# Threshold attention and a bilinear FFN on one core: later batches scored head by head, the FFN's first layer wholly in seven products, and the engines' orders taken from a list scheduler

## The chip, the cores and the metric

The kernel runs on one core of a Trainium2 chip. The core has a matmul engine (TensorE, "PE" in the profile, with its weight loads as "PEld"), a vector engine (VectorE, DVE), a scalar engine (ScalarE, ACT), a general engine (GpSimd, POOL) and an engine that here issues nearly all transfers (SyncE, SP). The metric is device time in microseconds, the median of several runs; lower is better. All data are 32-bit floats.

## The reference

```
scores = q @ k.T / 8                       # per batch b (8) and head h (8); 576 x 576, head size 64
thresh = max(scores, last axis) - tau
scores = where(scores >= thresh, scores, -1e9) - max
attn   = exp(scores); attn = attn / (sum(attn) + 1e-9)
x      = attn @ v, laid out as (8*576) tokens x (8*64) features
a, b   = x @ w_a, x @ w_b                  # 512 -> 1536 each
out    = (a * b) @ w_out                   # 1536 -> 512
```

So there is an attention of 64 heads with a hard threshold below each row's maximum, and after it an FFN on 4608 tokens whose hidden layer is the product of two linear maps.

## The kernel before

**Attention.** Work goes by pairs of heads (`pairs`, 32 of them, four to a batch) and by units: a unit (i, u) is 128 queries of pair i, or, for u = `NT`, the last 64 queries of two pairs. There are 144 units: 18 for the first batch, 126 for the other seven. One turn g of the main loop (a slot) starts unit g. `scores` (L389) multiplies queries by keys for both heads of the pair into two PSUM tiles `sc`, each 128 queries by 576 keys, and VectorE takes the row maxima (`mx`, L411) and the thresholds (`thr`, L412, one instruction for both heads). `weigh` (L422) lets ScalarE compute the exponentials into a room `tw` in SBUF (L431, L432), and VectorE select and sum them (L435). `reciprocal` (L440; L446, L448) and `normalise` (L451, L454) finish the rows. In the next slot `turn_blocks` (L493) transposes the room in 32x32 blocks on VectorE (L498) and posts four transfers that write it to DRAM (`swap`); `turn_back` (L513) posts those that read it back as `wT`. Three slots later `weighted` (L606) multiplies it by v (`product`, L542) and `settle` (L546) copies the result into `xT`: one copy on ScalarE (L549), two on VectorE (L550). The first eight units are transposed on the matmul engine instead (`turn_pe`, L468).

**FFN.** Tokens go in 18 blocks of 256. A matmul is a 64x64 tile of the array, and four of them, one in each quarter of the array, run beside each other; the profile shows each as two instructions, so a set of four is eight instructions. The first layer's 1536 columns are three groups of 512. For a block with four tiles of x (`x`, its copy with the two halves of the partitions exchanged `xS`, and two tiles of sums `xU` made by `x_sums`, L567), a group can be computed as a 2x2 block product by seven products instead of eight (`sevens_of`, L679; `product`, L709, matmuls at L720, 128 wide), which needs sums of weight quarters (`first_sums`, L669, L677). `SEVENS = 2` of the three groups go this way; the third goes through `plain` (L810, L824, 256 wide) piece by piece between the products. Only the last two blocks, those that begin after the attention (`state["over"]`), take all three groups by sevens, with the third group's weight sums in three rooms of `tw` (`last_rooms`). The second layer goes by seven products in 17 blocks (L885), with sums of h (`h_sums`, L861, L853) on GpSimd.

**Order.** The FFN is a generator whose steps `advance` (L969) hands out by columns, a share of a block in each slot (`PORTIONS`), so that FFN work lies between the steps of the attention. `keep_order` (L41) then ties each engine's instructions to the order in which the program wrote them. SP's transfers are posted to a list (`post`, L139) and handed to SP one by one as matmul columns go by (`passed`, L169; `pump`, L152), each behind a matmul.

**Rooms.** PSUM has four tiles of two banks (`banks`, L128) shared by scores, values, both FFN layers and transposes. `tw` has three buffers (`TW_BUFS`). The first slots also convert the weights from DRAM (L298 to L324).

Of the kernel before, what the change touches and what calls it, by code (L numbers as in the profile page):

```python
# [32 lines left out]
PART = 36864  # L33
PORTIONS = (0.3, 0.35, 0.15, 0.2)
RAWS = 4
TW_BUFS = 3
SEVENS = 2
BY_HEAD = 16


def keep_order(tc):  # L41

    last = {}
    for ins in tc.nc.cur_bb.bb.instructions:
        before = last.get(ins.engine)
        if before is not None:
            tc.add_manual_dep(
                ins, before,
                mybir.DependencyInfo(mybir.DependencyClass.NoSync, mybir.DependencyReason.DATA),
                reason="order")  # L50
        last[ins.engine] = ins.name
# [3 lines left out]
def kernel(  # L55
# [61 lines left out]

    def pool(name, bufs, **kw):
        return ctx.enter_context(tc.tile_pool(name=name, bufs=bufs, **kw))
# [32 lines left out]
    def pump(count=1, paced=True):  # L152

        for _ in range(min(count, len(bulk))):
            behind = next(x.name for x in reversed(nc.cur_bb.bb.instructions) if x.engine == mybir.EngineType.PE)
            for n, move in enumerate(bulk.pop(0)[2]):
                moved = nc.sync.dma_start(*move)
                if n == 0 and paced:
                    tc.add_manual_dep(
                        moved.ins, behind,  # L160
                        mybir.DependencyInfo(mybir.DependencyClass.Sync, mybir.DependencyReason.DATA),
                        reason="pace")
# [15 lines left out]
    def load(i, name):  # L178
# [6 lines left out]
        t = work.tile([P, most, Q], FP32, tag=name[0] + "T", bufs=bufs, name=name[0] + "T")[:, 0:n1 - n0]  # L185
        for j in range(2):
            rows = src[b, 2 * hp + j].rearrange("(e n) d -> e n d" if name == "k" else "(n e) d -> e n d", e=Q)
            moves = [(t[(2 * j + h) * Q:(2 * j + h + 1) * Q], rows[:, n0:n1, h * Q:(h + 1) * Q]) for h in range(2)]
            for some in ([moves] if name != "k" else [moves[0:1], moves[1:2]]):
                post((name, i), *some)  # L190
# [45 lines left out]
    for F in range(NF):  # L236
# [4 lines left out]
             "layer": False, "paced": False, "all": False, "turn": 0, "due": NPIECES, "wide": True, "slot": 0, "reading": False, "first": 0}  # L241
# [10 lines left out]
    more_sb = more_u32.bitcast(FP32)  # L252

    def load_weights(limit, engine=nc.sync, most=NPIECES):
# [4 lines left out]
        while most and (len(raws) - len(taken) < limit or extra) and state["loaded"] < state["due"]:  # L259
# [7 lines left out]
            for r, part in enumerate(src):  # L267
# [4 lines left out]
                if behind and r == 0:  # L272
                    tc.add_manual_dep(
# [58 lines left out]
    for _ in range(TW_BUFS):  # L332
        t = work.tile([P, 2 * NB, Q], FP32, tag="tw", bufs=TW_BUFS, name="rows")
        rooms.append(t.rearrange("p n e -> p (n e)")[0:R, 0:ROWS])
    rooms += [sums_sb[0:R, c:c + ROWS] for c in range(0, 5 * ROWS, ROWS)]
# [19 lines left out]
    prepared, scored, weights, turned, whole = {}, {}, {}, {}, {}  # L355
# [3 lines left out]
    last_sums = []  # L359
# [28 lines left out]

    def scores(i, u):  # L389
        qT, kT = prepared[i]["q" if i < HP else "q1" if u > 1 else "q0"], prepared[i]["k"]  # L390
        base = HALF if i >= HP and u > 1 else 0
        sc = [banks(SH, "sc") for _ in range(2)]
        wide = D if u == NT else columns()
# [3 lines left out]
        for c, t, j in each:  # L397
            r = slice(j * D, (j + 1) * D)
            if u < NT:
                m, o, q0 = j, t, u * P + t * D - base  # L400
            else:
                m, o, q0 = t, j ^ t, MAIN - base
                qT, kT = prepared[i + t]["q" if i < HP else "q1"], prepared[i + t]["k"]
            nc.tensor.matmul(sc[m][o * D:o * D + wide, c], qT[r, q0:q0 + wide],  # L404
                             kT[r, c * SH:(c + 1) * SH], start=True, stop=True)
        mx = small.tile([P, 2], FP32, tag="mx", name="mx")
        thr = small.tile([P, 2], FP32, tag="thr", name="thr")
        bias = small.tile([P, 2], FP32, tag="bias", name="bias")
        for j in range(2):
            c = slice(j, j + 1)  # L410
            nc.vector.tensor_reduce(mx[:, c], sc[j], axis=AX.XY, op=ALU.max)  # L411
        nc.vector.tensor_scalar(thr, mx, cut, None, op0=ALU.subtract)  # L412
        scored[i, u] = (sc, thr, bias, mx)

    def rooms_of(i, u):


        t = work.tile([P, 2 * NB, Q], FP32, tag="tw", bufs=TW_BUFS, name="tw")
        whole[i, u] = t
        return [t[:, j * NB:(j + 1) * NB] for j in range(2)]  # L420

    def weigh(i, u):  # L422

        sc, thr, bias, mx = scored.pop((i, u))
        n = len(sc)
        sums = small.tile([P, 2], FP32, tag="sums", name="sums")
        ws = rooms_of(i, u)
        sb = [s.rearrange("p c (n e) -> p c n e", e=Q) for s in sc]
        wb = [w.rearrange("p (c n) e -> p c n e", c=2) for w in ws]
        for j in range(n):  # L430
            nc.scalar.activation(bias[:, j:j + 1], mx[:, j:j + 1], AF.Copy, scale=e_nscale)  # L431
            nc.scalar.activation(wb[j], sb[j], AF.Exp, bias=bias[:, j:j + 1], scale=e_scale)  # L432
        for j in range(n):
            wv = wb[j]
            nc.vector.scalar_tensor_tensor(  # L435
                out=wv, in0=sb[j], scalar=thr[:, j:j + 1], in1=wv,
                op0=ALU.is_ge, op1=ALU.mult, accum_out=sums[:, j:j + 1])
        weights[i, u] = (ws, sums)
# [54 lines left out]
    def turn_blocks(i, u):  # L493

        ws, _ = weights.pop((i, u))
        t = whole.pop((i, u))
        for w in ws:
            nc.vector.transpose(w, w)  # L498
# [47 lines left out]
    def settle(out, pv, c0, c1, others):  # L546
# [3 lines left out]
        two = [nc.vector.tensor_copy(out[c * D:(c + 1) * D, n:2 * n], pv[(1 - c) * D:(2 - c) * D, 1, c0:c1])  # L550
               for c in range(2)]
# [23 lines left out]
    def exchange_blocks():  # L575
        while complete and not state["layer"] and not blocks:
# [5 lines left out]
            blocks.append(((x, xs) + ((x_sums(x), x_sums(xs)) if state["first"] >= 3 * SEVENS else ()), what))  # L582
# [76 lines left out]
    def sums_at(group, m):  # L659
        if group == SEVENS:  # L660
            return last_sums[m]
        return (first_sb, more_sb)[group][:, m * QUARTER:(m + 1) * QUARTER]

    def last_rooms():
        for _ in range(3):
            t = work.tile([P, 2 * NB, Q], FP32, tag="tw", bufs=TW_BUFS, name="s")
            last_sums.append(t.rearrange("p n e -> p (n e)")[:, 0:QUARTER])

    def first_sums(n, group):  # L669

        quarter = [w[:, NG - 1 - group].rearrange("p (z y e) w -> p z y (e w)", z=2, y=2)[:, :, y]
                   for w in (wa_sb, wb_sb) for y in range(2)]
        s1, s2, s4 = (sums_at(group, m).rearrange("p (z w) -> p z w", z=2) for m in range(3))
        a11, a12, a21, a22 = quarter
        out, a, b, op = ((s1, a21, a22, ALU.add), (s2, s1, a11, ALU.subtract), (s4, a12, s2, ALU.subtract),
                         (a21, a11, a21, ALU.subtract))[n]
        nc.gpsimd.tensor_tensor(out, a, b, op=op)  # L677

    def sevens_of(x, hg, plain):  # L679

        def pool(*a, **kw):
            (nc.vector if state["over"] else nc.gpsimd).tensor_tensor(*a, **kw)  # L682

        x, xs, t, ts = x

        everything = plain is None
# [6 lines left out]
        def s(m):  # L693
            return [[sums_at(NG - 1 - g, m)[:, k * CH:(k + 1) * CH] for k in range(HP)] if g >= of_all or everything
                    else None for g in range(NG)]
# [10 lines left out]
        nf = 2 * SEVENS  # L706
        two, one = range(of_all, NG), range(of_all)

        def product(m, out, fresh, last, groups=two):  # L709
            w, moving = products[m]  # L710
            nf = 2 * len(groups)
            left = whole = nf * HP * P
# [18 lines left out]

        (g0, g1), (h0, h1) = ([h[:, :, :, n * P:(n + 1) * P].rearrange("p f r n -> p r f n") for n in range(2)]
                              for h in hg)
        third = [work.tile([P, nf * P], FP32, tag="osb", bufs=OSB_BUFS, name="u3") for _ in range(2)]
        done = P, 0, 0

        if everything:
            last = work.tile([P, nf * P], FP32, tag="osb", bufs=OSB_BUFS, name="u3")
            n1, n2 = 2 * P * len(one), 2 * P * len(two)
            sets = [(two, n2, h0, h1, [t.rearrange("p (f n) -> p f n", n=P) for t in third]),  # L740
                    (one, n1, g0, g1, [last[:, r * n1:(r + 1) * n1].rearrange("p (f n) -> p f n", n=P)
                                       for r in range(2)])]
            pa, pb = {}, {}
            for m in (1, 2, 6, 5, 7, 3, 4):
                for groups, width, o0, o1, u in sets:
                    if m in (1, 2, 5):
                        (pa if m == 1 else pb)[width] = banks(width, "pab")
                    out = (pa if m in (1, 6, 7, 4) else pb)[width]
                    yield from product(m, out, m in (1, 2, 5), m in (2, 3, 4), groups)
                    ps = split(out)  # L750
                    if m in (1, 6):
                        nc.scalar.copy((o0, o1)[m == 6], ps)
                    elif m == 5:
                        for r in range(2):
                            nc.scalar.copy(u[r], ps[:, r])
                    elif m == 7:
                        for r in range(2):
                            nc.vector.tensor_tensor(u[r], u[r], ps[:, r], op=ALU.add)
                    else:
                        o = (o0, o1)[m == 3]  # L760
                        nc.vector.tensor_tensor(o, o, ps, op=ALU.mult if m == 4 else ALU.add)
                    if m == 3:
                        for r in range(2):
                            pool(o1[:, r], o1[:, r], u[r], op=ALU.mult)
                    yield done
            return
        a = banks(nf * P, "pab")
# [458 lines left out]
```

## Time and profile before

| | |
|---|---|
| median of 3 runs | 1419.35 us (1418.83 to 1419.81) |
| span of the profiled execution, the only time shown of it | 1417.0 us |
| busy: PE, PEld, DVE, ACT, POOL | 1370.2, 1229.6, 1013.7, 679.9, 495.7 us |
| mean granted TensorE clock | 0.994 |
| moved by DMA | 223.20 MB, 158 GB/s |
| matmul instructions, 128 wide in L720 / 256 wide in L824 / in L885 | 15232 / 4352 / 5712 |

The span is the time from the first to the last instruction of one execution, in which every busy time above lies. "Busy" is the union of an engine's instructions; for PE it is not the same as work at peak rate, since matmuls are pipelined and their ends are modelled. A group's line names the source line, the engine, the operation and the tiles, then the count, the busy time and the mean of one instruction. The chain of waits follows the work that ended last back to the start.

### The profile page before, as it was taken

The page shows a single profiled execution, that of the slowest core. Times are in us where ns is not written, and L with a number is a line of the kernel's source. Part 1 is how long each engine was busy: PE and PEld are TensorE (multiplying, and loading weights), DVE is VectorE, ACT ScalarE, POOL GpSimd, SP SyncE. Part 2 cuts the span into 40 slices and gives each one's busy share as a digit, 9 for nine tenths or more (in the row PEclk, how much of TensorE's full clock was granted, in tenths as well). Part 3 has the DMA queues.
Part 4 walks back from the last instruction along what each step waited for, and adds up shares of the span by engine and source line. Part 5 has one row for each costly group of instructions (what it writes and reads, how often), then busy time and mean ns, then how long its engine had stood idle before and what let it go on. Part 6 is the DMA issues. An engine that isn't in the chain of part 4 may idle for free.

```text
span 1417.0 us, 76257 instructions
## 1 busy us (share of the span) xinstructions
PE 1370.2 (97%) x33836; PEld 1229.6 (87%) x33836; DVE 1013.7 (72%) x2200; ACT 679.9 (48%) x1245; POOL 495.7 (35%) x678
## 2 busy tenths in 40 slices
PE   6788999999999999999999999999999999999998
PEld 5677579989878887979998999999888899799997
DVE  6898986778777877776767777677777776744424
ACT  5786554545445454545444545454545455431110
POOL 2674541606060606042333324150606060608100
PEclk9999999999999999999999999999999999999999
DMA  9967776667756775666555675567655775550000
GB/s 212 235 193 219 182 214 163 178 153 183 198 135 173 198 188 155 178 156 184 142 134 149 168 193 158 144 160 199 168 144 152 191 201 154 135 152 18 4 19 18
DMA packets 327000, 223.20 MB, mean 158 GB/s; under 512 B 171536, under 2 KB 310800, under 8 KB 326672
## 3 DMA queue, kind: packets, MB, share of 16 engines
q1 hardware_dynamic: 323712, 216.95, 59.2%
q8 instruction: 266, 4.36, 1.3%
q10 hardware_dynamic: 2960, 1.38, 0.4%
q14 instruction: 62, 0.51, 0.1%
HBM read 128.58 MB, written 89.65 MB: 154 GB/s over the span
## 4 chain that ended last, share of the span: by engine, by line
PE 86%; DVE 7%; DMA 3%; issue 2%; SPq 1%; ACT 0%; POOL 0%; DVEq 0%; POOLq 0%; ACTq 0%
PE pab L720 29%; PE po L885 20%; PE pab L824 16%; PE pv L542 10%; PE sc L404 10%; DVE mx L411 2%; DVE tw L498 2%; SPq L144 1%; DMA wT<-swap 1%; DVE tw L435 1%; PE tp L479 1%; DMA raw<-in_moe_w_a_dram 1%; DMA raw<-in_moe_w_b_dram 1%; DVE thr L412 0%; DVE u L790 0%
## 5 line engine op out<-in xcount | busy, mean ns | idle before, releaser
L411 DVE TENSOR_REDUCE mx<-sc 128x1 f32<-128x576 f32 x288 | 204.7, 752 | 125.8 <-PE sc L404 125.4
L454 ACT ACTIVATE tw<-tw,rcp 128x576 f32<-128x576 f32 x272 | 196.5, 770 | 202.3 <-DVE rcp L448 202.3
L682 POOL TENSOR_TENSOR h<-h,u 128x512 f32<-128x512 f32 x28 | 35.2, 1276 | 601.0 <-DVE h L794 426.1
L432 ACT ACTIVATE tw<-sc,bias,scalars 128x576 f32<-128x576 f32 x288 | 239.8, 833 | 10.9 <-PE pab L720 0.4
L435 DVE SCALAR_TENSOR_TENSOR tw<-sc,thr,tw 128x576 f32<-128x576 f32 x288 | 221.5, 799 | 10.4 <-ACT tw L432 9.9
L885 PE MATMUL po<-wo_sb,h 64*64 64x256 f32 x3264 | 205.8, 376 | 1.2 <-DVE h L794 1.1
L498 DVE STREAM_TRANSPOSE tw<-tw 128x576 f32<-128x576 f32 x272 | 194.4, 752 | 0.8 <-ACT tw L454 0.8
L885 PEld LDWEIGHTS po<-wo_sb,h 64*64 64x64 f32 x3264 | 157.0, 133 | 25.7 <-DVE h L794 2.6
L542 PE MATMUL pv<-wT,vm 64*64 64x160 f32 (+3 forms) x5184 | 169.2, 275 | 7.6 <-issue 3.6
L542 PEld LDWEIGHTS pv<-wT,vm 64*64 64x64 f32 x5184 | 157.4, 136 | 19.1 <-issue 9.8
L404 PE MATMUL sc<-kT,qT 64*64 64x288 f32 x2016 | 168.0, 404 | 1.1 <-DVE xt L550 0.5
L853 POOL TENSOR_TENSOR h<-h 128x256 f32<-128x256 f32 x168 | 117.4, 732 | 107.4 <-PE po L885 97.2
L885 PE MATMUL po<-sums_u,h 64*64 64x256 f32 x2448 | 153.4, 376 | 0.7 <-DVE h L832 0.7
L720 PE MATMUL pab<-xU,wb_sb 64*64 64x128 f32 x4352 | 138.0, 269 | 0.4 <-issue 0.3
L720 PEld LDWEIGHTS pab<-xU,wb_sb 64*64 64x64 f32 x4352 | 132.2, 133 | 3.7 <-issue 1.1
L885 PEld LDWEIGHTS po<-sums_u,h 64*64 64x64 f32 x2448 | 117.6, 133 | 19.4 <-DVE h L832 1.3
L404 PEld LDWEIGHTS sc<-kT,qT 64*64 64x64 f32 x2016 | 101.8, 133 | 22.6 <-issue 5.0
L549 ACT COPY xT<-pv 128x128 f32<-128x128 f32 (+1 forms) x68 | 17.7, 260 | 201.8 <-PE pv L542 200.2
L431 ACT ACTIVATE bias<-mx,scalars 128x1 f32<-128x1 f32 x288 | 83.1, 288 | 64.0 <-DVE mx L411 63.7
L550 DVE COPY xT<-pv 64x128 f32<-64x128 f32 (+1 forms) x136 | 38.1, 280 | 91.0 <-PE pv L542 89.7
L720 PE MATMUL pab<-xS,wa_sb 64*64 64x128 f32 x2176 | 101.8, 269 | 0.1
L531 ACT COPY kept<-po 128x512 f32<-128x512 f32 x65 | 34.8, 536 | 123.0 <-PE po L885 113.9
(156 smaller groups left out, 2414.3 us busy)
## 6 DMA issues: line engine op xcount, KB each, us to landing
wT<-swap SPq DMA_DIRECT2D x244, 288.0 KB, 3.9
swap<-tw SPq DMA_DIRECT2D x480, 144.0 KB, 2.9
vm<-in_v_dram SPq DMA_DIRECT2D x128, 72.0 KB, 2.5
swap<-tw SPq DMA_DIRECT2D x128, 72.0 KB, 3.0
kT<-in_k_dram SPq DMA_DIRECT2D x112, 72.0 KB, 3.3
wT<-swap SPq DMA_DIRECT2D x56, 144.0 KB, 3.3
out_dram<-kept SPq DMA_DIRECT2D x28, 256.0 KB, 3.9
qT<-in_q_dram SPq DMA_DIRECT2D x112, 40.0 KB, 2.8
```

The lines of the kernel that those rows point to most:

```text
L404: nc.tensor.matmul(sc[m][o * D:o * D + wide, c], qT[r, q0:q0 + wide], kT[r, c * SH:(c + 1) * SH], start=True, stop=True)
L411: nc.vector.tensor_reduce(mx[:, c], sc[j], axis=AX.XY, op=ALU.max)
L431: nc.scalar.activation(bias[:, j:j + 1], mx[:, j:j + 1], AF.Copy, scale=e_nscale)
L432: nc.scalar.activation(wb[j], sb[j], AF.Exp, bias=bias[:, j:j + 1], scale=e_scale)
L435: nc.vector.scalar_tensor_tensor(out=wv, in0=sb[j], scalar=thr[:, j:j + 1], in1=wv, op0=ALU.is_ge, op1=ALU.mult, accum_out=sums[:, j:j + 1])
L454: nc.scalar.activation(w, w, AF.Copy, scale=rcp[:, j:j + 1])
L498: nc.vector.transpose(w, w)
L542: nc.tensor.matmul(pv[c * D:(c + 1) * D, y], vm[rows, s], wT[y](rows, s), start=(s == 0), stop=(s == NSLOT - 1))
L720: nc.tensor.matmul(out[c * D:(c + 1) * D, r, f * P:(f + 1) * P], w[g][k][rows, w0:w0 + D], moving[k][rows], start=(fresh and k == 0 and f ...
L824: nc.tensor.matmul(pab[c:c + columns(), r], w[rows, f // n, k, fs + c:fs + c + columns()], moving, start=(k == 0), stop=(k == H - 1))
L853: (nc.vector if state["over"] else nc.gpsimd).tensor_tensor(*a, **kw)
L885: nc.tensor.matmul(po[c * D:(c + 1) * D, r, y], ht[rows, t0:t0 + D], other[rows, f], start=(f == 0), stop=(f == NF // 2 - 1))
```

## The change

1. **Scores by head.** In the seven later batches `scores_of` computes one head at a time into one `sc` tile, with the two halves of the keys on the two halves of the contraction rows; the half of the queries that is needed on the other partitions is copied there by ScalarE one slot earlier (`exchange_q`, tile `qx`, one buffer). Maximum, threshold, exponential and selection of head 0 come before the scores of head 1. The threshold is one instruction per head. `load` brings k in four transfers per head instead of two, each half as large. The slot's FFN shares follow `BY_HEADS`.
2. **First layer by seven in all three groups**, in all 16 blocks with four tiles. `plain` remains for the first two blocks. The steps of both layers are named (`T` two groups together, `O` the third, `F` the second layer) and run in the fixed order `ORDER`. The third group's sums have one buffer, `third_sb`, that is rewritten in place four times in a block (2, 4, "2", "1"). `tw` goes from three buffers to two; the rows of the first batch are loaded elsewhere. The FFN's new path starts after seven weight sums instead of six.
3. **`settle`** puts its two copies on ScalarE from slot 22 on.
4. **`order`** replaces `keep_order`: it simulates the program's instructions with a duration for each (`spent`, and formulas for matmuls and transfers), and for each engine it issues the instruction that is ready first among the next `LOOK` of the program (300 on PE, 24 on DVE and ACT, 12 on POOL, 1 on SP); the resulting orders are tied as before.

```diff
+ORDER = ("T1", "T2", "T6", "T5", "T7", "T3", "O1", "T4", "O2", "F4a", "O3", "F1a", "O4", "F2a", "F4b", "F1b", "F2b", "F5", "F7", "F6", "F3")
 PORTIONS = (0.3, 0.35, 0.15, 0.2)
+BY_HEADS = (0.25, 0.1, 0.2, 0.1)
-TW_BUFS = 3
+TW_BUFS = 2
+LOOK = {mybir.EngineType.PE: 300, mybir.EngineType.DVE: 24, mybir.EngineType.Activation: 24, mybir.EngineType.Pool: 12, mybir.EngineType.SP: 1}
+QX_BUFS = 1
...
+def spent(ins, outs, x, psum):
...
+    if len(ins) > 1 and n > 8:
+        more = 75 if len(ins) > 2 else 0
+        return (60 + 1.06 * n + more, 130 + 1.06 * n + more)
+    if n <= 8:
+        return (170, 170 + 60 * (len(ins) > 1))
+    return (75 + 1.04 * n, 150 + 1.04 * n)
...
+def order(tc, slots, paced, look):
...
+        best = None
+        for e, some in waiting.items():
...
+            limit = mine[min(ahead[e] + look[e], len(mine)) - 1]
+            pick = None
+            for n in some:
+                if n > limit:
+                    break
+                at = room(n)
+                if at is None:
+                    continue
+                at = max(at, ready[n], now[e])
+                if pick is None or at < pick[0]:
+                    pick = at, n, e
+                    if at <= now[e]:
+                        break
...
-            moves = [(t[(2 * j + h) * Q:(2 * j + h + 1) * Q], rows[:, n0:n1, h * Q:(h + 1) * Q]) for h in range(2)]
+                post((name, i), *((t[(2 * r + h) * Q:(2 * r + h + 1) * Q, j * NSLOT:(j + 1) * NSLOT],
+                                   rows[:, r * NSLOT:(r + 1) * NSLOT, h * Q:(h + 1) * Q]) for r in range(2) for h in range(2)))
...
+    def exchange_q(i, u):
+
+        t = work.tile([P, P], FP32, tag="qx", bufs=QX_BUFS, name="qx")
+        for m in range(2 if u == NT else 1):
+            qT, q0 = queries(i + m, u)
+            n = D if u == NT else P
+            for r in range(2):
+                nc.scalar.copy(t[r * D:(r + 1) * D, m * D:m * D + n], qT[(1 - r) * D:(2 - r) * D, q0:q0 + n])
+        exchanged[i, u] = t
...
+    def highest(i, u, heads):
+
+        sc, thr, bias, mx, sums = scored[i, u]
+        for j in heads:
+            nc.vector.tensor_reduce(mx[:, j:j + 1], sc[j], axis=AX.XY, op=ALU.max)
+        c = slice(heads[0], heads[-1] + 1)
+        nc.vector.tensor_scalar(thr[:, c], mx[:, c], cut, None, op0=ALU.subtract)
...
+    def scores_of(i, u, m):
...
+        for c in range(2):
+            j = m if u < NT else c ^ m
+            for r in range(2):
+                rows = slice(r * D, (r + 1) * D)
+                if r == j:
+                    mine = qT[rows, q0 + (c * D if u < NT else 0):][:, 0:D]
+                else:
+                    mine = qx[rows, (c if u < NT else m) * D:][:, 0:D]
+                nc.tensor.matmul(sc[c * D:(c + 1) * D, r], mine, kT[rows, j * SH:(j + 1) * SH], start=True, stop=True)
+        highest(i, u, (m,))
...
-        two = [nc.vector.tensor_copy(out[c * D:(c + 1) * D, n:2 * n], pv[(1 - c) * D:(2 - c) * D, 1, c0:c1])
-               for c in range(2)]
+        copy = nc.scalar.copy if state["slot"] > 18 + PV_LAG else nc.vector.tensor_copy
+        two = [copy(out[c * D:(c + 1) * D, n:2 * n], pv[(1 - c) * D:(2 - c) * D, 1, c0:c1]) for c in range(2)]
...
+        def of_one(n):
...
+            if n == 1:
+                yield from product(5, right, True, one, half)
+                first_sums("2", SEVENS)
+                yield P, half, 2 * half
+                yield from product(1, left, False, one)
+                at["v"] = temporary("u3").rearrange("p (r f n) -> p r f n", r=2, n=P)
+                nc.scalar.copy(g0, ps)
+                nc.scalar.copy(at["v"], qs)
+            elif n == 2:
+                yield from product(6, left, False, one)
+                nc.scalar.copy(g1, ps)
+                first_sums(4, SEVENS)
+            elif n == 3:
+                yield from product(7, left, False, one, half)
+                yield P, half, 2 * half
+                yield from product(3, right, False, one)
+                nc.vector.tensor_tensor(at["v"], at["v"], ps, op=ALU.add)
+                nc.vector.tensor_tensor(g1, g1, qs, op=ALU.add)
+                pool(g1, g1, at["v"], op=ALU.mult)
+            else:
+                yield from product(4, left, False, one, half)
+                yield P, half, 2 * half
+                yield from product(2, right, True, one)
+                nc.vector.tensor_tensor(g0, g0, qs, op=ALU.add)
+                nc.vector.tensor_tensor(g0, g0, ps, op=ALU.mult)
...
-            rest = [(f, 0, HALF, (w,)) for f in range((NG - SEVENS) * n) for w in both]
...
+            order = ORDER
+            parts_of = sevens_of(xT, h_of)
...
                     written(1, k14)
+                    if len(xT) == 4:
+                        first_sums("2", SEVENS)
+                        first_sums("1", SEVENS)
...
+            if by_head:
+                scores_of(i, u, 0)
...
-            advance(PORTIONS[0] * pace)
+            advance((BY_HEADS if by_head else PORTIONS)[0] * pace)
+        if by_head:
+            weigh(i, u, (0,))
...
+        if by_head:
+            advance(BY_HEADS[1] * pace)
+            scores_of(i, u, 1)
+            passed(S // 2)
+            following(g)
+            advance(BY_HEADS[2] * pace)
+            weigh(i, u, (1,))
...
-    keep_order(tc)
+    order(tc, slots, after_of, LOOK)
```

## The prediction

> **What bounds the kernel now.** I read the page's busy times and clock first, then its chain of waits by line, then busy times by stage, then the chain piece by piece, last the waits by engine.
>
> ```profile
> PE 1370.2 (97%) x33836; PEld 1229.6 (87%) x33836; DVE 1013.7 (72%) x2200; ACT 679.9 (48%) x1245; POOL 495.7 (35%) x678
> ...
> PE 86%; DVE 7%; DMA 3%; issue 2%; SPq 1%; ACT 0%; POOL 0%; DVEq 0%; POOLq 0%; ACTq 0%
> ```
>
> The chain is made of matmuls to 86%; no other engine is near full. By stage:
>
> ```profile
> 0.00:260.00 260.00, 228.39 (x4072) 192.79 (x4076) 213.40 (x471) 165.38 (x321) 126.73 (x143) 0.97 0.82 201
> 260.00:1282.00 1022.00, 1013.26 (x26085) 911.07 (x26080) 746.95 (x1638) 499.38 (x900) 336.77 (x495) 1.00 0.63 165
> 1282.00:1417.00 135.00, 128.54 (x3694) 125.69 (x3686) 53.32 (x92) 15.13 (x25) 32.19 (x42) 0.98 0.05 15
> ```
>
> The columns are the stretch, its length, busy PE, PEld, DVE, ACT and POOL, the granted clock, the DMA share and GB/s. The middle is the matmul engine's at a clock of 1.00; the start has 31.6 us without it (260 - 228.4), beside a VectorE that is 82% busy; the end is the FFN alone. Busy is not peak, so I price matmuls by undisturbed stretches of the chain (start, length, line, instructions):
>
> ```profile
> 1198.37 3.45 PE pab L824 x64
> ...
> 1233.58 3.49 PE pab L720 x128
> ```
>
> Instructions of 256 columns take 53.9 ns each, of 128 columns 27.3: a column costs nearly the same in both. A 288-wide score instruction takes 60.5 (16 in 0.97 us), one of L885 54.0, and values 34 or 27.3 by width. With the middle's counts (L720 12544, L824 3584, L885 4405, L404 1808, L542 2016 of 160 and 1728 of 128 columns) that is 342 + 193 + 238 + 109 + 69 + 47 = 998 of 1022 us. So some 24 us of the middle is waits and small gaps; the rest can only go if matmuls go.
>
> **The change, part by part.**
>
> *Third group by sevens.* In the middle L824 runs 3584 instructions: 14 blocks of 256, that is 193.2 us. In their place come 7 products x 2 x 4 x 4 matmuls x 2 instructions = 448 of 128 columns in a block, 6272 in all, 171.2 us. **-22.0 us**, on the path. The last two blocks already do it, the first two never do. Were the new matmuls followed by as many gaps as L720 could own at most (24 us over 12544, 1.9 ns each), 12 us would come back: -22 to -10. I take -22 and leave gaps to the next term.
>
> *Beside the matmuls, in the middle.* POOL gets four weight sums per block (L677, 2.37 us each) and one product of 512 columns (1.28, as L682): 14 x 10.8 = 151 us, 337 to 488. ACT gets the copies of queries: the middle has 114 units (228 exponentials), 13 of them for two pairs, so 254 copies, at most as long as L549's 128x128 (267 ns): 68 us; the moved copies of L550 (104 and 56, by L549's 267 and 192 ns): 38; one more eviction a block (0.58): 8. ACT goes from 499 to 613. DVE loses L550's 41 us and gets two more evictions a block (0.67 each, L832): +19. Its thresholds double, 113 to 226. Each engine stays below the matmuls, so I cost this at nothing; the cover is their idle share, and it is thinnest on DVE, because of the next view (start, length):
>
> ```profile
> 192.24 2.05 DVE L412 TENSOR_SCALAR thr<-mx,scalars 128x2 f32<-128x2 f32 x1
> ```
> ```profile
> 191.90 2.36 POOL L677 TENSOR_TENSOR more_u<-wb_sb 128x1024 f32<-128x1024 f32 x1
> ```
>
> A threshold that takes 228 ns at the median took 2.05 us here: it ended with the POOL instruction that began 0.3 us before it. Three such cases over 0.9 us are in the trace, each ending with a POOL instruction; maxima and transposes kept their 752 ns throughout. In the middle a threshold averages 319 ns (36.1 us / 113), a sum's (L446) 228 against 170. The change adds the long POOL instructions that do this. Weight sums will run 14 x 4 x 2.37 = 133 of some 1000 us; a threshold that meets one waits half of it on average, 1.19 us, so +158 ns on each: 226 x (319 + 158) = 108 us against 36, and 114 x 158 = 18 on L446. DVE: 747 - 41 + 19 + 72 + 18 = 815 of 1000, 82%. Still covered. [...] The scheduler's `spent` puts a threshold at 170 ns and knows nothing of it.
>
> *`third_sb`.* It is rewritten in place, so product 6 waits for sum "2", and that for product 5. Between 5 and 6 lie product 1 (64 instructions, 1.7 us) and T4 (128, 3.5 us) beside POOL's 2 x 1.28 + 2.37 = 4.9 us; 5.2 covers it barely, and any attention work in between adds to the cover. Without cover it is up to 2.4 us a block, 33 us. Nothing, then, and up to +33 for the range.
>
> *Two rooms `tw`.* From the first exponential of a unit to the issue of its last `swap` transfer the 114 units take 13.3 us on average (9 in 10 under 15.6), plus 2.9 to landing by the page's DMA table: a life of 16.2 us. Units follow each other every 8.77 us, so two rooms allow 17.5. One long life, in the timeline: exponentials at 604.23, selections only from 609.33 (two transposes and two FFN additions stood before them on DVE), transposes at 613.77, `swap` issues from 619.48 to 622.04. With before's times 30 of the 114 units would not have left their room by the time the next but one wants it, for 41 us in total. A waiting exponential holds every FFN eviction behind it on ACT, and those hold the matmuls. Against that, a scheduler that puts the selection right behind its exponential takes up to 4 us from a life. Bounds: 0 and +60. I take 0, since the third rival has the rest.
>
> *Transfers.* k comes in 224 issues of 36 KB in place of 112 of 72 KB, about 0.5 us of SP each (four `swap` issues take 2.05): +56 us of SP over 1100, behind which `swap` and `wT` wait, 0.4 us a unit. The bytes are the same, and DMA is 63% busy in the middle. Nothing.
>
> *Scores by head.* As many matmuls as before (four per head and half). A score tile is held for one head's maximum, threshold, exponential and selection rather than two heads', so a PSUM tile comes free earlier for the FFN.
>
> *The orders.* What can they fetch? In the middle, part of the 24 us. PE's and PEld's waits there that name a DVE or ACT eviction (u L790, h L794, L832, kept L532 and some xT) add up to some 17 us; a search over 300 matmuls could put other work before them, while the slower thresholds make new ones. Bounds: all 24 gained, or 35 lost (a third of a us in each of 114 units). I take a third of the 17: **-6 us**. At the start, 31.6 us of PE are idle; between 50 and 150 us DVE is busy for 44.7 and 43.4 of 50 each, so 12 us could go there before DVE is full; the first 50 us wait for transfers (DMA share 1.12), which no order changes. I take **-10**, bounds -25 (most of the idle) and +15 (two rooms here as well, with conversions on all engines). At the end 6.5 us are idle; the work is the same but for the sums on POOL. 0, bounds -4 and +4.
>
> **The sum.** 1417.0 - 22 - 6 - 10 = 1379 us of span. The median of the runs is 2.35 us over the profiled span, and I carry that: **1381 us**, 2.7% under 1419.35.
>
> **Rivals.**
> 1. *The orders fetch most of what idles.* -22, -18 in the middle, -22 at the start: 1357. For it: 31.6 idle us at the start, and a matmul engine that needs only something ready. Against it: DVE nearly full between 50 and 150 us, and durations in the scheduler that miss the held thresholds.
> [...]
> 3. *Two rooms bind: slower.* Head 0's exponential now runs ahead of head 1's by 0.3 of the slot's FFN work (about 6.8 us of a unit's 8.77, so 2.0) and one head's scores (0.5): 2.5 instead of 1.05 us. If DVE's and SP's parts of the life stay as they are, it is 16.2 + 1.5 + 0.4 = 18.1 us, and two rooms allow a unit every 9.05 us, where the forecast has 8.77 x 994/1022 = 8.53. 114 x 0.52 = 59 us. The search over 300 matmuls (600 instructions, 16 us at 27.3) can pull FFN work forward once; I take half of it: 1381 + 59 - 8 = 1432. From a life of about 17.7 us on (8.53 + 38/114 = 8.86 a unit) the kernel is slower than before. Against it: the 4 us in which selections stood behind other work.
> 4. *It doesn't do what it says:* seven weight sums instead of six must be through before the first block is prepared. They run one a slot before that block's attention is complete; one block late would cost 1.6 us. Inside every case.
>
> **Chances.** The forecast (1366 to 1398) 0.58, the first rival (1345 to 1366) 0.18, the second (1398 to 1425) 0.10, the third (1416 to 1470) 0.14. Leaving out 0.04 below 1350 and some 0.16 above 1414 gives the range **1350 to 1414**. Within 0.2%, about what can be told from no change, is 1416.5 to 1422.2. Faster: 0.58 + 0.18 + 0.08 = 0.84; within: 0.03; slower: 0.13.
>
> **What the profile after would show.** Right: no L824-like 256-wide first-layer instructions after the first two blocks, and 16 x 1344 = 21504 of 128 columns, still 27.3 ns each in long stretches; the middle's PE over 98% busy; POOL near 640 us, ACT near 800, thresholds at 400 to 550 ns. The first rival: PE busy over 240 of the first 260 us. [...] The third: ACT idle before exponentials, released by `swap` transfers. I am wrong if the matmuls' sum falls by 22 us and the span does not follow.

## The result, and the profile after

The changed kernel takes **1469.24 us** (median of 4 runs, 1463.79 to 1483.78) against 1419.58 us before: ratio 1.035, interval 1.0315 to 1.0387. It was forecast at 1381 us, 1350 to 1414, and is slower, outside the range. A second set of runs gave 1.0358 (e7). The profiled run took 1472.56 us, with a span of 1470.8 us at a clock of 0.984.

The page's busy times, and its line for the queue that brings TensorE's instructions (packets, MB, share of the engines):

```profile
PE 1383.5 (94%) x36524; PEld 1260.6 (86%) x36524; DVE 1060.1 (72%) x2176; ACT 815.1 (55%) x1705; POOL 667.4 (45%) x760
...
q8 instruction: 288, 4.72, 1.3%
```

The work is as predicted: 2688 more matmul instructions (6272 for 3584), POOL at 667 and ACT at 815 us (near 640 and 800 in the forecast). What differs is that PE idles more. By stage, in the columns of the prediction's table:

```profile
0.00:260.00 260.00, 229.15 (x3935) 194.62 (x3939) 218.87 (x465) 170.46 (x349) 127.49 (x138) 0.94 0.81 197
260.00:1336.00 1076.00, 1025.85 (x28855) 944.17 (x28850) 777.81 (x1629) 629.41 (x1331) 492.85 (x581) 0.99 0.61 158
1336.00:1470.00 134.00, 128.45 (x3752) 121.84 (x3744) 63.40 (x83) 15.19 (x26) 47.04 (x42) 0.99 0.05 16
```

The start has the same PE busy time in 260 us as before (229.2 against 228.4), the end is about the same, and the middle is 54 us longer. PE is idle there for 50 us, not 9. With the prediction's undisturbed prices, 260 to 1282 us holds 932 us of matmuls where the kernel before had 998: 90 us lost and not 24. The clock is a small part of these 66 us more: in the middle it fell to 0.50 in four stretches of 3.4 us (from 538, 876, 996 and 1163 us; in the kernel before in none), which is 6.8 us of full clock. PE's waits in the changed kernel (waiting line and tile, what released it, us in total, times, longest):

```profile
PE pab L1004 <- issue: 12.6, 20, 2.0
PE pv L833 <- issue: 9.5, 8, 2.2
...
PE pab L1004 <- DVE h L1075: 4.5, 4, 1.5
PE sc L701 <- DVE tw L722: 3.5, 5, 1.6
```

and the same view of the kernel before, for its FFN products:

```profile
PE pab L824 <- issue: 1.3, 2, 0.8
PE pab L720 <- issue: 1.2, 3, 0.6
```

No one wait carries the loss. Two things stand out: many short waits on VectorE, and stalls in the middle of a product that wait for nothing shown ("issue").

### The profile page after: what moved, and what is told of

The parts are those of the page before. It is cut to its first block, busy times and chain, and to the rows that moved or that the text cites. A ratio compares the mean times of both kernels' runs of the same rounds, so it can differ in the third digit from the quotient of the medians.

```text
span 1470.8 us, 82712 instructions
## 1 busy us (share of the span) xinstructions
PE 1383.5 (94%) x36524; PEld 1260.6 (86%) x36524; DVE 1060.1 (72%) x2176; ACT 815.1 (55%) x1705; POOL 667.4 (45%) x760
## 5 line engine op out<-in xcount | busy, mean ns | idle before, releaser
L720 ACT ACTIVATE tw<-sc,bias,scalars 128x576 f32<-128x576 f32 x288 | 238.3, 831 | 56.6 <-DMA swap<-tw 34.1
L1175 PE MATMUL po<-wo_sb,h 64*64 64x256 f32 x3264 | 220.9, 377 | 4.0 <-ACT xt L842 1.9
L1004 PE MATMUL pab<-xU,wb_sb 64*64 64x128 f32 x6144 | 202.5, 271 | 8.2 <-DVE h L1075 4.5
L967 POOL TENSOR_TENSOR h<-h,u 128x512 f32<-128x512 f32 x42 | 52.9, 1275 | 334.8 <-DVE h L1045 252.6
L1004 PEld LDWEIGHTS pab<-xU,wb_sb 64*64 64x64 f32 x6144 | 189.5, 134 | 16.9 <-DVE h L1075 7.2
L701 PE MATMUL sc<-kT,qT 64*64 64x288 f32 x1008 | 189.5, 410 | 6.5 <-DVE tw L722 3.5
L701 PE MATMUL sc<-kT,qx 64*64 64x288 f32 x1008 | 188.3, 411 | 6.5 <-DVE kept L823 1.6
L1175 PEld LDWEIGHTS po<-wo_sb,h 64*64 64x64 f32 x3264 | 161.7, 133 | 27.9 <-ACT xt L842 2.3
L1175 PE MATMUL po<-sums_u,h 64*64 64x256 f32 x2448 | 170.2, 376 | 0.3 <-issue 0.3
L1004 PE MATMUL pab<-xS,wa_sb 64*64 64x128 f32 x3072 | 145.6, 269 | 1.5 <-issue 1.4
L1175 PEld LDWEIGHTS po<-sums_u,h 64*64 64x64 f32 x2448 | 124.8, 133 | 17.2 <-issue 0.8
L1004 PE MATMUL pab<-xT,wa_sb 64*64 64x128 f32 x2688 | 125.3, 269 | 0.2 <-DVE kept L823 0.2
L1004 PEld LDWEIGHTS pab<-xS,wa_sb 64*64 64x64 f32 x3072 | 116.7, 133 | 4.1 <-issue 2.8
L964 POOL TENSOR_TENSOR third_sb<-wb_sb 128x1024 f32<-128x1024 f32 x33 | 78.2, 2369 | 74.1 <-PE pab L1004 74.0
```

Source lines behind the costliest of these rows:

```text
L701: nc.tensor.matmul(sc[c * D:(c + 1) * D, r], mine, kT[rows, j * SH:(j + 1) * SH], start=True, stop=True)
L720: nc.scalar.activation(w, s, AF.Exp, bias=bias[:, j:j + 1], scale=e_scale)
L1004: nc.tensor.matmul(out[c * D:(c + 1) * D, r, f * P:(f + 1) * P], w[g][k][rows, w0:w0 + D], moving[k][rows], start=(fresh and k == 0 and f ...
L1175: nc.tensor.matmul(po[c * D:(c + 1) * D, r, y], ht[rows, t0:t0 + D], other[rows, f], start=begun[pair] == 0, stop=begun[pair] == len(pair) ...
```

## The experiments

Ratios are to the kernel before on the same chip; 1% is 14.2 us.

### One part undone

Four theories named a part at fault: R the rooms, S the scheduler's orders, H head-by-head scoring, O the third group.

**e1** puts `keep_order(tc)` in place of `order(...)`. 

> The changed kernel with each engine's instructions tied in the order in which the program writes them, as the kernel before does it; nothing else is undone. Theory R (two rooms tw bind: 24 exponentials of the changed kernel wait 34 us for a swap transfer, and units follow each other every 9.22 us instead of 8.77): the order of the instructions is not the cause, so the time stays within 1% of the changed kernel, 1455 to 1485 us. Theory S (the scheduler's orders are the cause, since its durations differ from the chip's and an engine that waits in order holds what stands behind it): the time falls to between 1385 and 1425 us. Theory H (scoring head by head is the cause, one head's chain at a time): within 1% of the changed kernel, or slower, since the program's order of the heads is the least favourable one.

1512.23 us, 1.0607 (1.0579 to 1.0635). **e2** sets `by_head = False`, with k loaded as before. 

> The changed kernel with both heads scored together as in the kernel before (k loaded as before, no copies of the queries, thresholds for two heads in one instruction); scheduler, two rooms and the third group's sevens stay. R: a unit's two exponentials are again 1.05 us apart instead of 2.81, so a room's life is about 1.7 us shorter, about 14.5 instead of 16.2 us, under two periods; 1405 to 1440 us. S: no change, 1455 to 1485. H: 1385 to 1420.

1496.37 us, 1.0498 (1.0469 to 1.0527). Undoing either makes it slower, so S and H fall: within the changed kernel the scheduler wins 2.5% and scoring by head 1.4%. **e3** and **e4** make space with six x tiles and with the unit's small tiles (maxima, thresholds, bias, sums) put into one; e4 spends the space on a third room:

```diff
-XT_BUFS = 7
+XT_BUFS = 6        # e3, e4
-TW_BUFS = 2
+TW_BUFS = 3        # e4 alone
```


> The changed kernel with six buffers xT instead of seven and its small tiles (maximum, threshold, bias, sums) in one tile: the base for the next run, which needs the space. All theories: as the changed kernel, or a little slower for the missing xT, 1460 to 1490 us.

> As the run with six xT, but with three rooms tw instead of two; nothing else differs. R: no exponential waits for a swap transfer any more, units follow each other at 8.7 us or less, and the time is 40 to 60 us under the run with two rooms. S and H: within 10 us of it.

1507.52 (1.0577) and 1509.8 us (1.0591, 1.0553 to 1.0629). The exponentials of e3 waited 42.3 us in 30 for a transfer out of their room, those of e4 2.9 us in 2, and the time stayed: the third room is worth nothing here, so R falls. The space itself cost 2% (e3 against e7); the seventh x tile and the merged small tiles are not told apart.

**e5** computes the third group with 256-column products again (`of_one` is `yield from plain(n)`). 

> The changed kernel with the third group computed as before, in four pieces of 256 columns (in the places of O1 to O4), without its weight sums; head by head, scheduler and two rooms stay. After the first runs neither the orders, nor the two heads, nor the rooms explain the loss: undoing each of them made the kernel slower or changed nothing. Theory O (the third group by sevens makes the waits: its four steps hold one PSUM tile, wait for the sums in third_sb and put four long GpSimd instructions into each block): 22 us of matmuls come back, but 70 or more us of waits go; 1400 to 1425 us. Theory P (the waits come from everything together, PSUM and engines' queues are simply fuller): 1440 to 1470.

1465.61 us, 1.0327 (1.0304 to 1.0349). **e6** undoes both heads' scoring, the third group and the rooms, and keeps the scheduler. 

> Both heads together, third group plain, three rooms: the kernel before with the scheduler, the steps F in the order of the change, and settle's copies on ScalarE. O: 1395 to 1425 us, the scheduler alone gains or costs little. P: 1410 to 1440. If the scheduler's orders gain 30 us here as they do in the changed kernel: about 1395.

1474.31 us, 1.0397 (1.0351 to 1.0444). **e7** is the changed kernel again. 

> The changed kernel once more, on the chip of these runs, as their base; the kernel before took 1428 us on the chip of the last runs and 1420 on the first. All theories: 1.03 to 1.04 times the kernel before.

1471.98 us, 1.0358 (1.0321 to 1.0395). **e8** drops the four `first_sums` calls that rewrite `third_sb`. 

> The changed kernel, but third_sb is written once and not rewritten in each block (the four weight sums per block are left out, so products 6 and 3 of the third group use the wrong sums). The matmuls are the same. If O's waits come from the rewriting (waits for the sums, and some 150 us of GpSimd that hold VectorE): 1410 to 1435 us. If the rewriting is hidden: within 10 us of the changed kernel.

1466.23 us, 1.032 (1.0281 to 1.0359). O falls too: the third group by sevens is no faster than plain (the intervals of e5 and e7 overlap), and its sums on POOL account for some 6 us, which is within the spread of the runs. e6 has none of the named parts but the order and is no faster than the changed kernel. So the loss is in the scheduler or in what the change does beside its named parts.

### The scheduler and the step order apart

**f1** is the kernel before with `order` for `keep_order`. 

> The kernel before, unchanged in its work, buffers and steps, with one edit: the new scheduler sets the order of each engine in place of the program's order. Theory F (the scheduler is sound; what all slow variants share, the FFN's new step order and the x tiles held longer, costs the time): 1400 to 1420 us, no slower than before. Theory M (the scheduler packs each engine to a model that misses transfers, held VectorE instructions and instruction fetches, so that its order loses wherever it is used): 1440 to 1475 us.

1449.27 us, 1.0164 (1.0132 to 1.0196). **f2** is e6 with `keep_order`. 

> The kernel before with all that the changed kernel has but its three named parts: both heads scored together, the third FFN group plain, three rooms for weights, and each engine in program order; what is left of the change is the FFN's new step order, the settling copies on ScalarE, the merged loads of q and k, and the first rows in other rooms. Theory F: 1475 to 1515 us, since e6, the same with the scheduler, took 1474 and the scheduler gained some 38 us in the changed kernel. Theory M: 1420 to 1440 us, near before, since the scheduler would be what made e6 slow.

1500.31 us, 1.0518 (1.0478 to 1.0558). **f3** is f2 with one line changed:

```diff
-ORDER = ("T1", "T2", "T6", "T5", "T7", "T3", "O1", "T4", "O2", "F4a", "O3", "F1a", "O4", "F2a", ...)
+ORDER = ("T1", "T2", "T6", "O1", "T5", "T7", "T3", "O2", "T4", "O3", "O4", "F1", "F4", "F2", "F5", "F7", "F6", "F3")
```


> As f2, with one edit: the FFN's steps in the order that the kernel before has (all first-layer steps and their outputs ahead of the second layer's), in place of the new order that puts second-layer steps between. Theory F: 1420 to 1445 us, 40 us or more under f2. Theory M, or another of the common parts (settling copies on ScalarE, merged loads): within 15 us of f2.

1457.93 us, 1.0226 (1.0202 to 1.025). **f4** lets `settle` copy on VectorE in the changed kernel. 

> The changed kernel with one edit: the copies that bring a head's pv result out of PSUM, of which the change gives those of later units to ScalarE, all stand where the kernel before has them, half of them on VectorE. If ScalarE's added queue delays exponentials (the exponentials with their selects start about half of the stalls): 1440 to 1462 us. If not: within 6 us of the changed kernel (1464 to 1478 us), or slower, since VectorE is the busier engine.

1490.39 us, 1.0448 (1.0412 to 1.0485): the copies on ScalarE are a gain of about 1%. f1 and f2 each miss one theory's number: the scheduler costs 1.6% on the kernel before (against F), and without it the remainder costs 5.2% (against M). Both are true at once, and f3 finds 2.9% of the 5.2 in the step order. In f3 the first layer's steps still differ from those of the kernel before: T5, T7 and T3 stand ahead of T4, so two first-layer accumulators are open across an O step. **g1** puts them back, and with them the order of the copy into `at["u"]` and of the sum into it:

```diff
+ORDER = ("T1", "T2", "T6", "O1", "T7", "O2", "T4", "T5", "O3", "T3", "O4", "F1", "F4", ...)
-            elif m == 5:
+            elif m == 7:
...
-            elif m == 7:
+            elif m == 5:
```


> As f3 (program order, both heads together, plain third group), with one edit: the first layer's steps stand in exactly the order of the kernel before, T1 T2 T6 O1 T7 O2 T4 T5 O3 T3 O4, so that product 5's accumulator opens only when product 4 has closed the other one. f3 had T5 and T7 ahead of T4, with both accumulators open across an O step. Theory P (open accumulators take PSUM rooms from scores and pv): 1420 to 1435 us, ratio to before within 1.01. If the settling copies or the merged loads cost the 33 us of f3: 1445 to 1460.

**1424.37 us, 1.0002 (0.9979 to 1.0025).** All that f2 lost is the FFN's step order; the other common parts, taken together, cost nothing. The waits say in part how. PE's in g1:

```profile
PE pab L1085 <- DVE tw L726: 4.8, 5, 1.5
```

in f3, the same line:

```profile
PE pab L1085 <- DVE tw L726: 13.2, 13, 1.5
```

and in f2, where the second layer's steps stand between the third group's:

```profile
PE po L1149 <- DVE h L1093: 12.8, 6, 2.8
PE pab L1008 <- issue: 9.2, 19, 1.7
PE pab L1085 <- DVE tw L726: 8.2, 6, 3.2
PE pab L1085 <- DVE h L1049: 8.1, 3, 3.8
PE pab L1085 <- DVE h L1093: 6.6, 5, 2.5
```

A first-layer product reads nothing that a selection (L726) writes; it waits for the PSUM tile that the selection reads last. A second-layer product (`po`) waits for its data: it stands too close behind the eviction of `h`. These waits are a part of the loss: f3's on L726 grew by 8.4 us of the 33 that it loses. How long the four PSUM tiles were held, from the first matmul into a tile to its last reader, 300 to 1250 us, found by pairing the trace's instructions with the program's:

| | tiles held, mean of 4 | all four held | a `pab` tile, us | a `po` tile, us | ratio |
|---|---|---|---|---|---|
| before | 3.08 | 36% | 11.3 | 8.3 | 1 |
| g1 | 3.07 | 37% | 11.3 | 8.4 | 1.000 |
| f3 | 3.16 | 43% | 13.2 | 8.1 | 1.023 |
| f2 | 3.21 | 47% | 12.4 | 12.8 | 1.052 |
| changed | 3.32 | 43% | 23.6 | 13.1 | 1.036 |
| g2 | 3.15 | 35% | 23.2 | 9.9 | 1.051 |

**g2** tries the tiles in the changed kernel: O1, T4, O2, O3, O4, then the second layer whole. 

> The changed kernel with one edit: the second layer's first steps (F4a, F1a, F2a) no longer stand between the third group's steps; the second layer runs whole behind the first, F1 F4 F2 F5 F7 F6 F3. The scheduler stays. Theory P: a second-layer accumulator is then held some 8 us and not 13, so a room comes free earlier: 1440 to 1460 us. If the interleaving covers waits (for the sums of h on GpSimd) more than it takes rooms: 1475 to 1500.

1495.73 us, 1.0511 (1.0455 to 1.0567). Fewer tiles are held, and it is slower: theory P's number fails here. Second-layer products now wait 7.0 us in 6 for the evictions of `h` (`po L1175 <- DVE h L1082`; 1.4 in 2 in the changed kernel), and `issue` ahead of L1004 goes from 12.6 to 18.1 us: the interleaved steps cover some waits, and taking them out costs more than the tiles give. That the step order costs the time is shown for the kernel before's way of computing (f2, f3, g1). That it does so through PSUM tiles is shown for those waits of f3 and only argued beyond: f2 and g2 have the same ratio, with 3.21 and 3.15 tiles held.

### Instruction fetch

**g3** changes only the width in the kernel before: each first-layer `plain` matmul of 256 columns becomes two of 128, each with its own weight load, in the blocks with four tiles of x.

```diff
+                        for z in range(cut):
+                            for r in range(2):
...
-                                nc.tensor.matmul(pab[c:c + columns(), r],
+                                    nc.tensor.matmul(pab[c:c + columns(), r, z * n1:z * n1 + n1],
```


> The kernel before with one edit: each 256-column product of the third group is issued as two of 128 columns, in all 3584 more matmuls in the profile with the same columns in all (2 x 27.3 ns against 53.9 ns). Theory I (TensorE is held by instruction fetch where its instructions are short): 8 to 20 us slower than before, with more idle put down to nothing but issue. If fetch does not bind: within 4 us of before.

**1473.99 us, 1.0343 (1.0303 to 1.0384)**, far above theory I's own 8 to 20 us, for the same columns and the same work on every other engine. Its instruction queue and PE's waits:

```profile
q8 instruction: 294, 4.82, 1.4%
```
```profile
PE pab L720 <- issue: 14.8, 26, 1.5
PE pab L827 <- issue: 14.7, 21, 2.0
```

It has 28 packets and 0.46 MB more than before's 266 and 4.36 for 7168 more instructions (3584 matmuls, each with a weight load): 256 instructions and 16 KB in each. 128 matmuls of 27.3 ns take 3.49 us, so by estimate TensorE uses up a packet in 3.49 us in a run of 128-column products, and in 6.9 in a run of 256-column products (128 of 53.9 ns). In g3 46 idle stretches of PE and PEld together (over 150 ns, 150 to 1280 us) end 1.1 to 1.7 us after the end of such a packet, with no instruction of VectorE, ScalarE or GpSimd ending in the 60 ns before; they make 27.3 us. The kernel before has 4 of 1.4 us, the changed kernel 17 of 11.6, e7 23 of 11.4, e5 22 of 10.7. In g3 the packets of these stalls came late: counted in TensorE's instructions they began some 60 later (median) than the packets of that stretch do, and 4.67 us (median) after the one before. Packets can follow each other faster: 28 began within 3.6 us of the one before, and only 2 of these are followed by such a stall. So the stalls do not show a highest rate of fetching, and why some packets come late stays open. The other 20 us that g3 loses lie in smaller gaps of the same lines, not assigned one by one; that they are fetch too is not shown, and neither is that the added weight loads have no part in them.

The step order may lose by this too. By the same count f2 has 24 stalls of 11.6 us, f3 8 of 3.3 and g1 8 of 4.9; the new order puts six products of 128-column steps in a row (T1, T2, T6, T5, T7, T3), where the old one has 256-column steps between them. No run separates the fetch from the tiles there.

### Parts alone, on the old step order

**g4** is e5 with g1's step order. 

> As e5 (changed kernel with a plain third group, head-by-head scoring, scheduler), with the FFN's steps in exactly the order of the kernel before. e5 took 1465.61. Theory P: 1430 to 1448 us, since the scheduler and head-by-head scoring then have the free rooms of before, less what the scheduler's order loses of itself (24 us in f1). If the step order matters only in program order: within 8 us of e5.

1456.08 us, 1.021 (1.0174 to 1.0245): 1.2% better than e5, less than P's forecast. **i1** is g1 with scoring by head, its loads and its two rooms. 

> As g1 (program order, old step order, plain third group: as fast as before), with one part of the change put in: head-by-head scoring with its merged loads and two rooms for weights. If head-by-head scoring is free, or a gain where the step order leaves rooms (e2 to e7 gave 20 us for it): 1400 to 1425 us. If two rooms or the second pass over scores cost (the rival that the prediction priced at 1432 for both): 1430 to 1450 us.

1459.83 us, 1.0256 (1.0232 to 1.0279). ScalarE's waits in i1:

```profile
ACT tw L732 <- DMA swap<-tw: 56.2, 29, 4.6
```

This is the third rival's sign, exponentials that wait for a room; the changed kernel has 34.1 us in 24. Three rooms do not fit beside seven x tiles, so rooms and the second pass over the scores are not told apart here. **i2** gives f1's scheduler a margin:

```diff
-            ready[m] = max(ready[m], (at + busy if same else end + 60))
+            ready[m] = max(ready[m], (at + busy if same else end + 300))
```


> As f1 (the kernel before, scheduler in place of program order, 1449.27), with one number of the scheduler changed: a result counts as ready for another engine 300 ns after its end and not 60 ns. If f1 loses because its orders are packed to times that the chip doesn't keep: 1425 to 1440 us. If it loses by the reordering itself, whatever the margin: 1443 to 1456 us.

1449.56 us, 1.018 (1.0162 to 1.0198). A margin of 300 ns changes nothing, so f1 does not lose by packing too tightly to this degree, and the reordering itself is what is left. f1's largest new wait on PE is `sc L633 <- DVE xt L779`, 9.3 us in 5: scores pulled ahead wait for a tile that a copy of values has yet to free. What a better rule for choosing would be was not tried.

## Why the prediction was wrong

Adding the parts one after another, in ratios: g1 1.000; the new step order 1.052 (f2); the scheduler 1.040 (e6); scoring by head and two rooms 1.033 (e5); the third group by sevens 1.036 (e7). In this order 74 us are lost in one line, `ORDER`, which belongs to the change and has no term in the prediction, and the parts that it priced bring back 23 of them. The shares hang on the order of adding: on the old step order the scheduler alone costs 1.6% (f1), scoring by head and two rooms 2.6% (i1), all of these together 2.1% (g4), and the new step order then adds 1.2% (e5 against g4). The third group by sevens on the old step order was not run.

- **The step that failed** is "Beside the matmuls, in the middle": it counted engines' busy shares, found each with room and costed the rest at nothing, and "The orders" bounded what the middle could lose more at 35 us. The middle lost 66 us more, 90 for 24. The change also decides in what order TensorE meets its products, and so how long accumulators stay open, how close a step stands behind the one that it reads, and how many narrow products stand in a row; busy shares show none of this. That is f2 against g1, +5.2%, and +1.2% beside the scheduler and scoring by head. The sentence "I am wrong if the matmuls' sum falls by 22 us and the span does not follow" is what happened.
- **Third group, -22 us.** The count came (21504 of 128 columns), the gain did not: e7 is 4 us over e5, which the intervals do not tell from none. The bound on gaps, 1.9 ns a matmul, was taken from a kernel in which 256-column products lay between the 128-column ones. In the middle L1004's instructions (17472 up to 1282 us) lost 64 us, 3.7 ns each, against 1.3 in L720, counted from the start of one instruction to the start of the next. In g3 narrow products lost time by themselves, 27 of the 48 us in stalls behind late packets; in the changed kernel, which stalls for other reasons too, the share of fetch in those 64 us is not settled.
- **`third_sb` and two rooms, nothing.** e8 and e4 bear that out: some 6 us within the spread of the runs, and none with six x tiles.
- **Scores by head, a tile free earlier.** In the changed kernel it wins: -1.4% (e2 against e7). Alone on the old order, with two rooms, it costs 2.6% (i1), with the waits of the third rival.
- **The orders, -6 and -10 us.** On the kernel before they cost 24 us (f1). The prediction bounded the middle at 35 lost and chose the sign by the waits that a search could fill; that scores pulled ahead must wait for tiles (9.3 us in f1) was not counted. In the changed kernel `order` does win, 35 us over e1, but against a program order that the change itself had made 6.1% slower. PE's busy time at the start did not move (229.2 us in 260).
- **Thresholds and sums behind POOL** were priced alike, 158 ns more on each. Of these and the maxima, only those with two columns were held in the changed kernel: the 252 thresholds of one column take 217 ns at most and the 288 maxima 759, while the sums go up to 2404 and the 18 thresholds of two columns to 1015. By lines, of the changed kernel (busy us, mean ns, idle before):

```profile
L658 DVE TENSOR_SCALAR thr<-mx,scalars 128x1 f32<-128x1 f32 (+1 forms) x270 | 60.7, 225 | 8.3
L734 DVE TENSOR_SCALAR sums<-sums 128x2 f32<-128x2 f32 x136 | 55.7, 409 | 4.0
```

and the kernel before:

```profile
L412 DVE TENSOR_SCALAR thr<-mx,scalars 128x2 f32<-128x2 f32 x144 | 50.6, 351 | 5.1
...
L446 DVE TENSOR_SCALAR sums<-sums 128x2 f32<-128x2 f32 x136 | 32.1, 236 | 3.3
```

The thresholds came down, from 351 ns to 225 on average, 212 where by head they have one column. In e2, where they have two again beside the same sums on POOL, 144 of them take 405 ns on average and up to 2297. The sums' 158 ns were about right: 236 became 409, in e7 346.
- **The third rival** has the measured time in its range (1416 to 1470), but by luck: without the waits for a room the time stayed (e3, e4).

## What to carry to other kernels

The order in which a program meets its accumulators is a change of its own: list what is open in PSUM at each step before and after, and price a step that stands right behind the one it reads. Where the matmul engine is the bound, count its instructions as well as its columns: here the same columns in twice as many instructions cost 48 us (g3). A scheduler has to be measured on the best program order known, not on one made for it.

## What the hardware showed that was not expected

- **Narrow matmuls stalled behind late packets of instructions**: 3584 instructions of 256 columns cut in halves cost 48 us, 27 of them in 46 stalls that end 1.1 to 1.7 us behind the end of such a packet (g3).
- **The one-column thresholds were not held by GpSimd.** In the changed kernel 252 `tensor_scalar` of 128x1 (thresholds) take 212 ns on average and 217 at most, though 31 of them lie inside a GpSimd instruction that runs on for more than 0.5 us after their end. The 136 of 128x2 (sums) go up to 2404, and the 11 of them over 900 ns each end within 0.03 us of the end of a GpSimd instruction; without the weight sums (e8) these 136 fall from 409 ns (346 in e7) to 283 and the thresholds stay at 212. With two columns thresholds were held as well: in e2 11 of 144 take over 900 ns, and each ends with a GpSimd instruction. Why one column escapes is not shown.
